# Every fourth attention head: V held still in TensorE, probabilities streamed past it

## The chip, the cores and the metric

The kernel runs on one core of one Trainium2 chip. The metric is the device time of one execution in microseconds, and the median of several executions is what is compared. TensorE does the matrix products, ScalarE (ACT) the exponentials, VectorE (DVE) the evacuations of PSUM and the elementwise work, GpSimd (POOL) a few scalars and some DMA issues, and SyncE (SP) most DMA issues.

## The reference

What is computed, cut to what matters here: a layer norm, an attention block over 32 heads with 2048 queries and 2048 cached keys, an MLP with a squared ReLU whose SiLU gates the attention's output, and a residual.

```python
xn = _layernorm(x)                        # x: 1 x 2048 x 512
q = (xn @ wq)                             # to 32 heads x 2048 x 128
scores = einsum("bhqd,bhkd->bhqk", q, k_cache) * (128 ** -0.5)
p = softmax(scores)                       # over 2048 keys
o = einsum("bhqk,bhkd->bhqd", p, v_cache)
s = o.reshape(1, 2048, 4096) @ wo         # to 512
h = relu(xn @ w1 + b1) ** 2               # 512 to 1792
g = silu(h @ w2 + b2)                     # back to 512
out = x + s * g
```

## The kernel before

**Tiling.** The 2048 queries are cut into 4 blocks of 512 (`QB`). A "group" g is one head of one block, so there are 128 groups (`NG`), g = 32 * block + head. The 2048 keys of a group are cut into 16 tiles of 128, taken two at a time: 8 "pairs" (`NPR`) a group, 1024 pairs (`NPAIR`) in all. One pass of the main loop (line 963) is one pair `pi`, called a step here.

**What one step puts on TensorE, in this order.** `gen_scores(pi)` (line 528): two matmuls of 512 columns, with a K tile stationary and the 512 queries moving, into one half of `psA`; behind them ACT's exponential of the 128x1024 result into `pT` (line 550 on), one of `NPT` = 4 buffers. Then none to three "fill" matmuls of 512 columns (`fill_one`, line 793): pieces of the Q projections, the MLP and the output projection, taken from a list of jobs in order of due step and paced by a credit, so that they last to the end. They go to the two banks of `psF`; a job's bank is evacuated by DVE, and two jobs later the bank is used again. Last, `gen_pv(pi - 2)` (line 559): the product of the probabilities with V, two steps behind the scores (`LAG`).

**The product with V before the change.** A pair takes 8 matmuls: for each of its two key tiles and each of 4 tiles of 128 queries, the 128x128 block of `pT` is the stationary operand and the V tile is the moving one. V has an extra column of ones (`Dh + 1` = 129 columns), so that column 128 of the result is the softmax's denominator. The 4 query tiles lie in two banks of `psO`, two to a bank. The helper `_mm_shared` (line 157) issues them; all other matmuls go through `_mm` (line 152). In a group's first and last pair the matmuls of bank 0 come before those of bank 1. After the last pair DVE copies the two banks to `o_un` (helper line 179), takes the reciprocal of the denominators (line 183), and multiplies into `o_bf` (line 165); `gen_oT` then has SP transpose `o_bf` by DMA into `oT`, which is what the output projection (`job_wo`) reads. `oT` has 24 slots (`NOT`).

**What orders the work.** All five instruction streams are written out by this program in order; each engine takes its own strictly in that order, and waits on counters of other engines and of DMAs. So an instruction on DVE that waits for something late holds all that is behind it on DVE. An exponential waits for its scores and for the product that last read its `pT` buffer. Scores of pair `pi` wait for the exponential of `pi - 2`, since `psA` holds two pairs. A group's first product into a bank of `psO` waits for that bank's copy.

**Layer norm of the next block.** `ln_transpose` (line 380) has SP transpose the normalised rows by DMA into `xnT`, which holds all 2048 queries.

```python
        if pi >= NPR:
            gen_pv(pi - LAG)
        if k == 0:
            fill_wq(g + 3)
            fill_k(g + 2)
        if k == LAG - 1:
            fill_v(g + 2)
        if k == LAG + 1 and g >= 1:
            gen_oT(g - 1)
```

Of the kernel before, what the change touches and what calls it, by code (L numbers as in the profile page):

```python
# [4 lines left out]

ACT = mybir.ActivationFunctionType
ALU = mybir.AluOpType
BF16 = mybir.dt.bfloat16
F32 = mybir.dt.float32
P = 128  # L10
# [193 lines left out]
    return e.bn_aggr(out, in_)  # L204


def _dma(e, out, in_):
    return e.dma_start(out, in_)  # L208

# [5 lines left out]
def bass_recurrent_scan__mha_block_cached__dense_activation_squared_relu__prompt_kernel(  # L215
# [13 lines left out]
    _, Sq, D = A_x.shape  # L229
# [3 lines left out]
    QB = 512  # L233
# [11 lines left out]
    HC = 8  # L245
# [12 lines left out]
    E = S.emit  # L258

    sb = nc.alloc_sbuf_tensor  # L260
    NSL, NSW, NQS, NPT, NOT = 3, 4, 3, 4, 3 * HC
    xnT = sb("xnT", [P, NDC, Sq], BF16)
    w1_sb = sb("w1_sb", [P, NDC, F], BF16)
    w2_sb = sb("w2_sb", [P, NFC, D], BF16)
    wo_all = sb("wo_all", [P, H, D], BF16)
# [9 lines left out]
    o_un = sb("o_un", [P, 2, TPB, Dh + 2], F32)  # L275
    rden = sb("rden", [P, 2, TPB], F32)
    o_bf = sb("o_bf", [P, 2, TPB, Dh], BF16)
    r_t = sb("r_t", [P, 2, QB], BF16)
    z_t = sb("z_t", [P, 2, D], F32)
    th_t = sb("th_t", [P, 2, D], BF16)  # L280
# [8 lines left out]
    ve_t = sb("ve_t", [P, TPB], F32)  # L289
    mhalf = sb("mhalf", [P, 1], F32)  # L290
    ident = sb("ident", [P, P], BF16)
    identf = sb("identf", [P, P], F32)
    warm = sb("warm", [P, P], BF16)
    rstd = sb("rstd", [P, TPB], F32)
    x_t = sb("x_t", [P, TPB, D], BF16)
    tmp_t = sb("tmp_t", [P, 2, D], F32)
    out_t = sb("out_t", [P, 2, D], BF16)

    psA = nc.alloc_psum_tensor("psA", [P, 4 * 512], F32)
# [6 lines left out]
    def bankO(i):  # L306
# [15 lines left out]
    sl_xt = [S.slot(f"xt{i}") for i in range(TPB)]  # L322
    sl_out = [S.slot("out0"), S.slot("out1")]
    sl_fin = [S.slot("fin0"), S.slot("fin1")]

    t_warm = E(GP, partial(_memset, out=warm[:], val=0.0))
    t_mhalf = E(GP, partial(_memset, out=mhalf[:], val=-0.5))
    t_idf = E(GP, partial(_iota, out=identf[:]))
    t_ident = E(GP, partial(_ts, out=ident[:], in0=identf[:], scalar1=0.0, scalar2=None,
                            op0=ALU.is_equal), deps=[t_idf])  # L330
    t_ones = None
    for i in range(NSL):
# [4 lines left out]


    t_xl = {}
    t_xn = {}  # L340
    t_xr = {}
    t_xnr = {}
# [37 lines left out]
    def ln_transpose(j, i):  # L380
        jt = j * TPB + i
        t_xnr[jt] = tok_xT[j][i] = S.emit_dma(
            SP, partial(_dmaT, out=xnT[:, :, jt * P:(jt + 1) * P], in_=xn_t[:, i, :]),
            sl_xT[i], deps=[t_xn[jt]])

    def ln_next(j, i):
        ln_scale(j, i)
# [140 lines left out]
    def gen_scores(pi):  # L528
        g, k = divmod(pi, NPR)
        s2, i = pi % 2, g % NSL  # L530
        assert t_kfill[g] is not None and t_evac[g] is not None
        t = None
        if g == 0:
            qt, b = divmod(pi, 2)
            for c in range(NKT // 2):
                t = E(PE, partial(_mm_shared, out=psA[:, s2 * 1024 + c * P:s2 * 1024 + (c + 1) * P],
                                  lhsT=kT[:, 0, (b * NKT // 2 + c) * P:(b * NKT // 2 + c + 1) * P],
                                  rhs=qt_sb[:, 0, qt * P:(qt + 1) * P], start=True, stop=True),
                      deps=[t_k0[b], t_q0[qt], t_exp[pi - 2] if pi >= 2 else t_b1[0]],
                      inc=(c == NKT // 2 - 1))  # L540
        else:
            for n in range(2):
                tt = 2 * k + n
                t = E(PE, partial(_mm, out=psA[:, s2 * 1024 + n * 512:s2 * 1024 + (n + 1) * 512],
                                  lhsT=kT[:, i, tt * P:(tt + 1) * P], rhs=qt_sb[:, g % NQS, :],
                                  start=True, stop=True),
                      deps=[t_exp[pi - 2] if pi >= 2 else None, t_kfill[g], t_evac[g],
                            t_bankF[0] if pi == 0 else None],
                      inc=(n == 1))
        if k == NPR - 1:  # L550
            t_S_last[g] = t
        t_exp[pi] = E(AC, partial(_act, out=pT[:, pi % NPT, :],
                                  in_=psA[:, s2 * 1024:(s2 + 1) * 1024],
                                  func=ACT.Exp, scale=SM_SCALE),
                      deps=[t, t_PV[pi - NPT] if pi >= NPT else None])

    t_bank = [None, None]

    def gen_pv(pi):
        g, k = divmod(pi, NPR)  # L560
        i = g % NSL
        last = k == NPR - 1
        if k == 0:
            t_bank[:] = [None, None]
        order = [(2 * k + n, qt, n * QB + qt * P) for n in range(2) for qt in range(TPB)]
        if last or k == 0:
            order = [(2 * k + n, qt, n * QB + qt * P) for b in range(2)
                     for qt in (2 * b, 2 * b + 1) for n in range(2)]
        if g == 0:
            order = [(k % 2 * (NKT // 2) + n, k // 2, n * P) for n in range(NKT // 2)]  # L570
        t = None
        for idx, (tt, qt, p0) in enumerate(order):
            b = qt // 2
            inc = idx == 7 or (last and g > 0 and idx == 3)
            t = E(PE, partial(_mm_shared, out=bankO(b)[:, qt % 2 * 256:qt % 2 * 256 + Dh + 1],
                              lhsT=pT[:, pi % NPT, p0:p0 + P],
                              rhs=v_sb[:, i, tt, 0:Dh + 1],
                              start=(tt == 0 and qt % 2 == 0), stop=(tt == NKT - 1)),
                  deps=[t_exp[pi], t_v0[k % 2] if g == 0 else t_vfill[g], t_ones,
                        t_evac[1] if g == 0 and b == 1 else None,  # L580
                        t_oev[g - 1][b] if g >= 1 else None], inc=inc)
            if inc:
                t_bank[b] = t
        t_PV[pi] = t
        if last:
            t_PV_last[g] = t
            s = g % 2
            for b in range(2):
                t_oev[g][b] = E(DV, partial(_copy, out=o_un[:, s, 2 * b:2 * b + 2, 0:Dh + 1],
                                            in_=bankO(b).rearrange("p (s c) -> p s c", s=2)[:, :, 0:Dh + 1]),  # L590
                                deps=[t_bank[b], t_onorm[g - 2] if g >= 2 else None])
            tr = E(DV, partial(_recip, out=rden[:, s, :], in_=o_un[:, s, :, Dh]),
                   deps=[t_oev[g][0], t_oev[g][1], t_onorm[g - 2] if g >= 2 else None])
            base = rden[:, s, :]
            rb = bass.AP(tensor=base.tensor, offset=base.offset,
                         ap=[list(base.ap[0]), [1, TPB], [0, Dh]])
            t_onorm[g] = E(DV, partial(_tt, out=o_bf[:, s, :, :], in0=o_un[:, s, :, 0:Dh], in1=rb,
                                       op=ALU.mult),
                           deps=[tr, tok_oT[g - 2] if g >= 2 else None])

    def gen_oT(g):
        tok_oT[g] = S.emit_dma(
            SP, partial(_dmaT, out=oT[:, g % NOT, :].rearrange("p (t q) -> p t q", q=P),
                        in_=o_bf[:, g % 2, :, :].rearrange("p t d -> p (t d)")), sl_oT[g % 4],
            deps=[t_onorm[g], t_wodone[g - NOT] if g >= NOT else None])
# [12 lines left out]
    t_zrd = [None, None]  # L618
    t_thr = [None, None]
    events = {}  # L620
    nfin = [0]

    pending = []
# [3 lines left out]

    def job_proj(g):
        j = g // H
        js = slice(j * QB, (j + 1) * QB)  # L630
        i = g % NSW

        def mm(n, bank):
            t = E(PE, partial(_mm, out=bankF(bank), lhsT=wq_sb[:, i, n, :], rhs=xnT[:, n, js],
                              start=(n == 0), stop=(n == NDC - 1)),
                  deps=[t_wqfill[g], t_bankF[bank]] + tok_xT[j], inc=(n == NDC - 1))
            assert t_wqfill[g] is not None and None not in tok_xT[j]
            if t is not None:
                t_proj[g] = t

        def evac(bank, step):
            t_evac[g] = E(DV, partial(_copy, out=qt_sb[:, g % NQS, :], in_=bankF(bank)),
                          deps=[t_proj[g], t_S_last[g - NQS] if g >= NQS else None])
            return t_evac[g]
        return NDC, mm, evac

    def job_h(j, c):
        js = slice(j * QB, (j + 1) * QB)
        box = [None]

        def mm(n, bank):
            box[0] = E(PE, partial(_mm, out=bankF(bank), lhsT=w1_sb[:, n, c * P:(c + 1) * P],
                                   rhs=xnT[:, n, js], start=(n == 0), stop=(n == NDC - 1)),
                       deps=[tok_w1[c // 2], t_bankF[bank]] + tok_xT[j], inc=(n == NDC - 1))

        def evac(bank, step):
            s = c % 2
# [305 lines left out]
    for pi in range(NPAIR):  # L963
# [17 lines left out]
            n += 1  # L981
        if pi >= NPR:
            gen_pv(pi - LAG)
        if k == 0:
            fill_wq(g + 3)
            fill_k(g + 2)
# [17 lines left out]
        step += 1  # L1004
    while tail_order:
        tail_one(step)
    assert not jobs and cur[0] is None and not events and not pending

    fin = [_Tok(sl.sem, sl.val) for sl in sl_out + sl_fin]
    S.emit_wait(SP, fin)  # L1010
# [29 lines left out]
```

The softmax here doesn't subtract the row's maximum and nothing guards it: scores larger than these inputs give would overflow.

## Time and profile before

| what | value |
|---|---|
| median of 4 runs | 1238.13 us (1237.68 to 1238.33) |
| the profiled execution | 1238.26 us, span 1236.5 us |
| exponentials, 128x1024 | 1024 of 1024 ns each |
| products with V, 129 columns | 8192 matmuls |
| score matmuls, 512 columns | 2032 (and 64 of 128 columns at the start) |
| fill matmuls, 512 columns | 504 + 480 + 224 + 224 in `psF`, 16 at the end in `psA` |
| tanh on ACT, 128x512 | 16, 622 ns each |
| load on the 16 DMA engines | 80.4% of 16 engines by the queue that SP, mostly, feeds; 1.1% by POOL's |

How to read it: TensorE's records are modelled at their ends and overlap (a 512-column matmul has 379 ns in the records), so its cost is read from the distance between starts. The span covers the instructions; the execution's own time is 1.8 us longer. A group lasts about 1236.5 / 128 = 9.66 us and a step 1.21 us.

### The profile page before, as it was taken

To read this page: it belongs to the slowest core of one execution; us is meant where nothing else is said; L and a number is where in the kernel's file an instruction comes from. 1 tells how busy PE (TensorE), PEld (TensorE's weight loads), DVE (VectorE), ACT (ScalarE), POOL (GpSimd) and SP (SyncE) were. 2 spreads that over 40 slices of the span, in tenths; PEclk is the share of its full clock that TensorE was granted. 3 is DMA by queue.
4 is the path that set the end of the run, shared out by engine and by line. 5 is a ranking of instruction groups with operands and counts; after the bars stand their busy time and mean duration, and the time that the engine had idled before them with its cause. 6 is when DMAs were issued, how large, how long until landed. Compare 5 with 4: busy or idle time off the path is not lost.

```text
span 1236.5 us, 26934 instructions
## 1 busy us (share of the span) xinstructions
PE 1232.1 (100%) x11885; PEld 819.5 (66%) x11885; DVE 472.7 (38%) x953; ACT 1054.6 (85%) x1044; POOL 32.0 (3%) x73
## 2 busy tenths in 40 slices
PE   9999999999999999999999999999999999999999
PEld 7666666666666666666666666666666666666665
DVE  4453323244435332334444532333344333324333
ACT  7888888888888888888888888888888888888885
POOL 1010000000002000000000200000000000000000
DMA  9999998677879898767778888787778789878761
GB/s 210 206 233 202 187 179 134 130 144 142 141 151 173 142 158 131 140 139 145 134 132 171 171 139 143 141 148 134 133 146 148 146 154 158 137 135 146 145 122 31
DMA packets 686868, 185.41 MB, mean 150 GB/s; under 512 B 673536, under 2 KB 685568, under 8 KB 686752
## 3 DMA queue, kind: packets, MB, share of 16 engines
q1 hardware_dynamic: 684656, 179.62, 80.4%
q0 software_dynamic: 1424, 3.81, 1.1%
q8 instruction: 94, 1.54, 0.6%
q10 hardware_dynamic: 672, 0.26, 0.1%
q14 instruction: 22, 0.18, 0.1%
HBM read 96.60 MB, written 2.10 MB: 80 GB/s over the span
## 4 chain that ended last, share of the span: by engine, by line
PE 99%; DMA 0%; DVE 0%; issue 0%; SPq 0%; DVEq 0%
PE psO L157 38%; PE psA L152 36%; PE psF L152 25%; DMA kT<-in_A_k_cache_dram 0%; PE psA L157 0%; PE psO L196 0%; DVE out_t L165 0%; PE psF L196 0%; DVE tmp_t L175 0%; PE psO L152 0%; DVE xnT L179 0%; SPq L208 0%; PE psA L196 0%; DVEq L119 0%
## 5 line engine op out<-in xcount | busy, mean ns | idle before, releaser
L161 ACT ACTIVATE pT<-psA 128x1024 bf16<-128x1024 f32 x1024 | 1044.5, 1024 | 162.5 <-PE psA L152 117.6
L157 PEld LDWEIGHTS psO<-v_sb,pT 128*128 128x128 bf16 x8192 | 547.9, 98 | 240.2 <-issue 12.4
L157 PE MATMUL psO<-v_sb,pT 128*128 128x129 bf16 x8192 | 631.2, 220 | 0.0
L152 PE MATMUL psA<-qt_sb,kT 128*128 128x512 bf16 x2032 | 604.4, 379 | 0.0
L179 DVE COPY o_un<-psO 128x258 f32<-128x258 f32 x256 | 97.4, 422 | 399.4 <-PE psO L157 398.7
L152 PE MATMUL psF<-xnT,wq_sb 128*128 128x512 bf16 (+1 forms) x520 | 168.8, 374 | 0.1
L152 PE MATMUL psF<-wo_all,oT 128*128 128x512 bf16 x480 | 163.7, 379 | 0.0
L152 PEld LDWEIGHTS psA<-qt_sb,kT 128*128 128x128 bf16 x2032 | 157.0, 98 | 0.0
L179 DVE CAST qt_sb<-psF 128x512 bf16<-128x512 f32 (+1 forms) x130 | 88.0, 677 | 97.5 <-PE psF L152 97.5
L165 DVE TENSOR_TENSOR o_bf<-o_un,rden 128x512 bf16<-128x512 f32 x128 | 88.6, 692 | 4.6 <-DVE rden L183 0.3
L152 PEld LDWEIGHTS psF<-xnT,wq_sb 128*128 128x128 bf16 x520 | 50.3, 98 | 59.8 <-DVE xnT L179 0.2
L171 DVE TENSOR_SCALAR r_t<-psF,b1f 128x512 bf16<-128x512 f32 x56 | 42.0, 750 | 117.5 <-PE psF L152 117.5
L152 PEld LDWEIGHTS psF<-wo_all,oT 128*128 128x128 bf16 x480 | 46.9, 98 | 56.4
L152 PE MATMUL psF<-xnT,w_sb 128*128 128x512 bf16 x224 | 77.1, 379 | 0.0
L152 PE MATMUL psF<-w_sb,h2T 128*128 128x512 bf16 x224 | 74.1, 379 | 0.0
L152 PEld LDWEIGHTS psF<-w_sb,h2T 128*128 128x128 bf16 x224 | 21.9, 98 | 26.4
L152 PEld LDWEIGHTS psF<-xnT,w_sb 128*128 128x128 bf16 x224 | 21.9, 98 | 26.4
L165 DVE TENSOR_TENSOR z_t<-psF,b2bc 128x512 f32<-128x512 f32 x16 | 11.1, 692 | 67.2 <-PE psF L152 67.2
L165 DVE TENSOR_TENSOR acc<-psF,acc 128x512 f32<-128x512 f32 x28 | 19.3, 689 | 30.0 <-PE psF L152 30.0
L208 POOL DMA_DIRECT2D out_dram<-out_t x12 | 6.7, 557 | 891.0 <-DVE out_t L165 891.0
L165 DVE TENSOR_TENSOR h2T<-r_t 128x512 bf16<-128x512 bf16 x56 | 23.8, 425 | 1.9
L183 DVE RECIPROCAL rden<-o_un 128x4 f32<-128x4 f32 x128 | 22.9, 179 | 4.4
(47 smaller groups left out, 166.3 us busy)
## 6 DMA issues: line engine op xcount, KB each, us to landing
v_sb<-in_A_v_cache_dram SPq DMA_DIRECT2D x127, 512.0 KB, 4.7
wq_sb<-in_A_wq_dram SPq DMA_DIRECT2D x127, 128.0 KB, 3.0
wo_all<-in_A_wo_dram SPq DMA_DIRECT2D x4, 1024.0 KB, 6.2
w_sb<-in_B_w_dram SPq DMA_DIRECT2D x14, 256.0 KB, 4.8
oT<-o_bf SPq DMA_TRANSPOSE x128, 4.0
x_t<-in_A_x_dram POOLq DMA_DIRECT2D x16, 128.0 KB, 3.2
kT<-in_A_k_cache_dram SPq DMA_TRANSPOSE x127, 4.5
x_ln<-in_A_x_dram SPq DMA_DIRECT2D x15, 128.0 KB, 4.3
```

The lines of the kernel that those rows point to most:

```text
L152: return e.matmul(out, lhsT, rhs, start=start, stop=stop)
L157: return e.matmul(out, lhsT, rhs, start=start, stop=stop, skip_group_check=True)
L161: return e.activation(out, in_, func, bias=bias, scale=scale)
L165: return e.tensor_tensor(out, in0, in1, op)
L171: return e.tensor_scalar(out, in0, scalar1=scalar1, scalar2=scalar2, op0=op0, op1=op1)
L179: return e.tensor_copy(out, in_)
L183: return e.reciprocal(out, in_)
L208: return e.dma_start(out, in_)
```

## The change

Of the 128 groups, those with `g % 4 == 1` and `4 < g < 126` are handled in a second way ("B groups" here, the others "A groups"): g = 5, 9, ..., 125, which are 31. Both ways compute the same.

In a B group a pair's product takes 2 matmuls: the V tile (128 columns, no ones) is stationary, and 512 probabilities of `pT` move past it. The result is o transposed, 128x512, in bank 0 of `psO` alone. ACT copies it to `o_un`. The denominators are not in it any more: DVE reads every `pT` pair of the group with a reduction that transposes 32x32 blocks (`den_part`, 8 a group, 128x1024 each), sums the parts (`den_sum`), writes 128x16 sums to DRAM over POOL's DMA queue, reads them back by 4 DMAs so that each group of 32 partitions holds all four quarters, sums these, takes the reciprocal and spreads it by a DVE transpose (`den_spread`), and multiplies into `oT` directly (`den_scale`). There is no DMA transpose of `o_bf` for a B group.

`plan_b` fixes the steps after whose product these are emitted: the parts at steps 8g + 2 + (0, 1, 3, 4, 6, 7, 9, 10), the sum at 8g + 14, the spread at 8g + 21, the scaling at 8g + 22. The group after a B group does its first pair's bank 0 products one step later, between the bank 1 and the bank 0 products of its second pair. There are 8 `pT` buffers in place of 4, and an exponential also waits for the part that reads its buffer. `xnT` holds two blocks in place of four (its DMA transposes then wait for the last use of the block before last), and `identf` lies in `tmp_t`.

```diff
-    NSL, NSW, NQS, NPT, NOT = 3, 4, 3, 4, 3 * HC
-    xnT = sb("xnT", [P, NDC, Sq], BF16)
+    NSL, NSW, NQS, NPT, NOT = 3, 4, 3, 8, 3 * HC
+    xnT = sb("xnT", [P, NDC, 2 * QB], BF16)
...
+    def is_b(g):
+        return g % 4 == 1 and 4 < g < NG - 2
...
-            sl_xT[i], deps=[t_xn[jt]])
+            sl_xT[i], deps=[t_xn[jt], t_xuse.get(j - 2)])
...
-                      deps=[t, t_PV[pi - NPT] if pi >= NPT else None])
+                      deps=[t, t_PV[pi - NPT] if pi >= NPT else None, t_part.get(pi - NPT)])
...
+    def gen_pv_b(pi):
+        g, k = divmod(pi, NPR)
+        i = g % NSL
+        for n in range(2):
+            tt = 2 * k + n
+            t_PV[pi] = E(PE, partial(_mm, out=bankO(0), lhsT=v_sb[:, i, tt, 0:Dh],
+                                     rhs=pT[:, pi % NPT, n * QB:(n + 1) * QB],
+                                     start=(tt == 0), stop=(tt == NKT - 1)),
+                         deps=[t_exp[pi], t_vfill[g], t_free[0]], inc=(n == 1))
+        if k == NPR - 1:
+            t_PV_last[g] = t_PV[pi]
+            t_free[0] = E(AC, partial(_act, out=o_b(g), in_=bankO(0), func=ACT.Copy),
+                          deps=[t_PV[pi], t_onorm[g - 2]])
...
+    def den_part(pi):
+        k = pi % NPR
+        t_part[pi] = E(DV, partial(_reduce_t, out=d_part[:, k, :],
+                                   in_=pT[:, pi % NPT, :].rearrange("p (b j) -> p b j", j=32)),
+                       deps=[t_exp[pi], t_den[0]])
+
+    def den_sum(g):
+        t_den[0] = E(DV, partial(_reduce, out=d_sum[:],
+                                 in_=d_part[:].rearrange("p k (n b) -> p b (k n)", n=2)),
+                     deps=[t_part[NPR * (g + 1) - 1], t_den[1]])
+        t_den[1] = S.emit_dma(GP, partial(_dma, out=d_scr, in_=d_sum[:]), sl_dw,
+                              deps=[t_den[0], t_den[2]])
+        src = bass.AP(tensor=d_scr.tensor, offset=d_scr.offset,
+                      ap=[[NBK, 32], [32 * NBK, 4], [1, NBK]])
+        free = [t_den[1], t_den[3]]
+        for a in range(4):
+            t_den[2] = S.emit_dma(GP, partial(_dma, out=d_quad[32 * a:32 * (a + 1), :, :],
+                                              in_=src), sl_dr, deps=free)
+
+    def den_spread(g):
+        t_den[3] = E(DV, partial(_reduce, out=d_rec[:],
+                                 in_=d_quad[:].rearrange("p a b -> p b a")),
+                     deps=[t_den[2], t_den[5]])
+        t_den[4] = E(DV, partial(_recip, out=d_rec[:], in_=d_rec[:]), deps=[t_den[3]])
...
+        t_den[5] = E(DV, partial(_transpose32, out=r_all[:], in_=spread),
+                     deps=[t_den[4], t_den[5]])
+
+    def den_scale(g):
+        t_onorm[g] = tok_oT[g] = E(
+            DV, partial(_tt, out=oT[:, g % NOT, :], in0=o_b(g),
+                        in1=r_all[:].rearrange("p b i -> p (b i)"), op=ALU.mult),
+            deps=[t_free[0], t_den[5], t_wodone[g - NOT] if g >= NOT else None])
+
+    def plan_b(g):
+        first = NPR * g + LAG
+        for k in range(NPR):
+            at_once.setdefault(first + 3 * k // 2, []).append(partial(den_part, NPR * g + k))
+        at_once.setdefault(first + 12, []).append(partial(den_sum, g))
+        at_once.setdefault(first + 19, []).append(partial(den_spread, g))
+        at_once.setdefault(first + 20, []).append(partial(den_scale, g))
...
+        if after_b and k == 0:
+            later[:] = order[:4]
+            order = order[4:]
+        if after_b and k == 1:
+            order = [x for x in order if x[2] >= 2] + later + [x for x in order if x[2] < 2]
...
+        if k == 0 and is_b(g):
+            plan_b(g)
+        for fn in at_once.pop(pi, []):
+            fn()
```

The helpers `_reduce_t` and `_reduce` are `tensor_reduce` with an add over the last axis, the first with `apply_transpose=True`; `_transpose32` is DVE's `transpose`.

## The prediction

> **What bounds the kernel now.** I read the page's busy shares first, then the chain that ended last, then the timeline of TensorE.
>
> ```profile
> span 1236.5 us, 26934 instructions
> ...
> PE 1232.1 (100%) x11885; PEld 819.5 (66%) x11885; DVE 472.7 (38%) x953; ACT 1054.6 (85%) x1044; POOL 32.0 (3%) x73
> ...
> PE 99%; DMA 0%; DVE 0%; issue 0%; SPq 0%; DVEq 0%
> ```
>
> TensorE never stops, and the chain that set the end is 99% TensorE. So two things alone can move the time: fewer TensorE nanoseconds, or a new wait on TensorE. For the nanoseconds I need the pitch from start to start, since records overlap. This is TensorE's timeline late in the run (start us, length us, engine, line, operation, tiles, shape, count):
>
> ```profile
> 1208.77 0.59 PE L152 MATMUL psA<-qt_sb,kT 128*128 128x512 bf16 x2
> 1209.20 0.38 PE L152 MATMUL psF<-wo_all,oT 128*128 128x512 bf16 x1
> 1209.41 0.62 PE L157 MATMUL psO<-v_sb,pT 128*128 128x129 bf16 x8
> 1209.87 0.59 PE L152 MATMUL psA<-qt_sb,kT 128*128 128x512 bf16 x2
> 1210.30 0.62 PE L157 MATMUL psO<-v_sb,pT 128*128 128x129 bf16 x8
> 1210.75 0.59 PE L152 MATMUL psA<-qt_sb,kT 128*128 128x512 bf16 x2
> ```
>
> Two score matmuls take 1209.20 - 1208.77 = 0.43 us, one fill 0.21, eight products 0.455. Over the 13 steps from 1206.56 to 1220.23 there are 36 matmuls of 512 columns and 104 of 129: at 0.2158 us for the first, the second come to (13.67 - 7.77) / 104 = 0.0567 us. Check: 8192 x 0.0567 + some 3,490 x 0.2158 = 1218 us, and the start and the end make up the rest. Weight loads (98 ns each) are hidden at both pitches.
>
> **The gain.** A pair of a B group drops 8 x 0.0567 = 0.4536 us and adds 2 x 0.2158 = 0.4316 (the price of the score matmuls, the same shape with a new weight load each): 0.022 us. Times 8 pairs it is 0.176 us a group, times 31 groups **5.5 us**. The two pairs after a B group are only reordered. [...]
>
> So 0.176 us a group is the whole stake: a wait of that size on TensorE in each B group eats it. The rest is a search for waits.
>
> **DVE's new work.** Its rows:
>
> ```profile
> L179 DVE COPY o_un<-psO 128x258 f32<-128x258 f32 x256 | 97.4, 422 | 399.4 <-PE psO L157 398.7
> L165 DVE TENSOR_TENSOR o_bf<-o_un,rden 128x512 bf16<-128x512 f32 x128 | 88.6, 692 | 4.6 <-DVE rden L183 0.3
> ...
> L183 DVE RECIPROCAL rden<-o_un 128x4 f32<-128x4 f32 x128 | 22.9, 179 | 4.4
> ...
> L200 DVE BATCH_NORM_STATS2 st_t<-x_ln 128x6 f32<-128x512 bf16 x15 | 10.2, 682 | 3.5 <-DMA x_ln<-in_A_x_dram 3.5
> ...
> L200 DVE BATCH_NORM_STATS2 st_t<-x_ln 128x6 f32<-128x256 bf16 x2 | 0.8, 420 | 0.0
> ```
>
> Removed in a B group: 2 x 0.422 + 0.179 + 0.692 = 1.71 us. Added: the part, a reduction over 1024 bf16 elements with a transpose, has no row. The nearest is the statistics row, also a reduction: (682 - 420) / 256 = 1.02 ns an element, so 0.682 + 512 x 1.02 = 1.21 us. The lower bound is two elements at a time, by the bf16 row of `xn_t` (406 ns for 512): about 0.7 us; the upper, that the transpose halves the rate: 2.25. I take 1.21. Eight make 9.7; the sum over 256 elements 0.42 (the 256 row), over 64 some 0.22, reciprocal 0.18, transpose and scaling of 512 as the 692 row each. Sum 11.9, net +10.2 us a group, x 31 = 315: DVE goes from 473 to about 788 us (64%). That it hides rests on three places. [...]
>
> *The `pT` buffers.* Part 0 can start when the group before is normalised, at about step 8g + 3.3. The exponential of pair 8g + 15 waits for part 7, at about step 8g + 15.5: 12.2 steps x 1.2 us = 14.6 us for eight parts and some 2 us of other DVE work. Records on DVE overlap by 0.08 us (two copies of 0.42 take 0.76), so 8 x 1.13 + 2 = 11 us: 3.6 us to spare.
>
> *Evacuations behind a part.* From the end of a `psF` evacuation to the first matmul that needs that bank again the trace has at least 0.94 us, and over 1.8 us in 19 of 20. A part holds one back by at most 1.13 us, mostly less, since the parts run ahead of their places whenever DVE has nothing to wait for. `psO` copies are tighter: bank 1's end only 0.14 us before its next use. But A copies are emitted at steps 8g + 1, 8g + 17, 8g + 25, and between part 7 (8g + 12) and 8g + 17 DVE catches up. I allow 0.4 us over the whole run.
>
> *The trip through DRAM.* POOL's rows:
>
> ```profile
> L208 POOL DMA_DIRECT2D x_t<-in_A_x_dram x16: 538/538/616, 89.1 to 1015.8; - x16
> ...
> DMA to landing us min/median/max: 2.3/3.2/5.1
> ```
>
> POOL's writes to `out` land in 2.0 to 4.0 us, median 2.3. Write 2.3, handoff 0.1, the fourth read issued 3 x 0.54 = 1.6 later, landing 3.2: 7.2 us; bounds 5.9 and, with 4.0 and 5.1, 10.8. Packets of 64 bytes have no row; `b1b`, 3.5 KB, took 4.7, which for both ends makes 11.1. From the sum to the spread there are 7 steps, 8.4 us. If it is late, DVE stands at the spread. The next evacuation behind it (step 8g + 22, ready at 22.9) has 8.9 x 1.2 = 10.7 us from the sum's step, less 0.4 for the sum and 1.6 for spread and scaling, plus 1.8 slack: 10.5. The copies of group g + 2, at the end of step 8g + 25, give (11.9 x 1.2) - 2.0 = 12.3. So it is covered, with a margin of 3 to 5 us. POOL's other work (layer norm scalars 30 steps ahead of use, output issues) can bear that wait. For g = 125 the last fill of the loop, which reads this `oT` slot, runs in step 1023 (1220.66 us in the trace), one step after the scaling; DVE is idle there for 6.5 us, so parts and sum come early.
>
> **ACT's new work.** One copy of 128x512 from PSUM a B group, between two exponentials. The trace has the same insertion sixteen times, the tanh:
>
> ```profile
> 1195.09 1.02 ACT L161 ACTIVATE pT<-psA 128x1024 bf16<-128x1024 f32 x1 [0.29 <-PE psA L152]
> 1196.01 0.62 ACT L161 ACTIVATE th_t<-z_t 128x512 bf16<-128x512 f32 x1
> 1196.53 1.02 ACT L161 ACTIVATE pT<-psA 128x1024 bf16<-128x1024 f32 x1
> ```
>
> It holds the next exponential by 0.52 us, which ends at 1197.55; TensorE starts the scores that need it at 1197.97, with no gap. Over the sixteen the least slack left is 0.33 us. The copy's product is done before the exponential in front of it ends. ACT rises by 31 x 0.62 = 19 us to 1074 (87%). If the cover were gone, 0.52 x 31 = 16 us.
>
> **Moved and dropped.** SP loses 31 DMA transposes of `oT` and gains nothing; a transpose of `xnT` now waits for uses that ended some 80 steps before. `oT` of a B group is there at 8g + 23, the earliest output job that reads it is released 16 steps on. These cost nothing.
>
> **The sum.** 1238.26 (the profiled execution; the median is 0.13 lower) - 5.5 + 0.4 = 1233.2; against the median **1233.0 us**. The floor is the gain with no wait, 1232.6, less run scatter: 1232.0.
>
> **Rivals.** A measurement of this kernel can tell about 0.2% (2.5 us) from no change.
>
> *Small waits eat it* (0.13). Evacuations behind parts, or the ACT copy, cost about 0.1 to 0.25 us a group: 31 x 0.18 = 5.5, so 1236 to 1240, middle 1238. For: the `psO` copies have 0.14 us. Against: the schedule keeps parts off those steps, and the tanh rows.
>
> *The parts are too slow* (0.06, slower). Place: the exponential of pair 8g + 15, held by part 7; its point is 8c + 2 = 14.6 + 0.5 of slack, c = 1.6 us a part. At 2.25 it is 8 x 0.65 = 5.2 us a group, 161 us: 1394. For: no transposing row. Against: the statistics row is 0.4 us below the point.
>
> *The DRAM trip* (0.08, slower). DVE stands at the spread until the reads land; it decides from 10.5 to 12.3 us. At 14 us it costs (14 - 12.3) x 31 = 53: 1285. For: `b1b`'s 4.7 us, and the DMA engines are 80% busy with large loads. Against: every loaded POOL row in mid-run is under 5.1.
>
> *The change doesn't save* (0.02, slower). The V loads are not hidden: 16 x 0.098 x 31 = 49 us, 1281. Against: the score matmuls do just that at 216 ns.
>
> **Numbers.** The forecast has 0.71, and it is all of "faster" (below 1235.65); small waits make "same", 0.13; the other three "slower", 0.16. The range runs from 1232.0 into the small waits, to 1238.5; about 0.2 lies above. The forecast's own range is 1232.0 to 1235.
>
> **What would show it.** Right: TensorE's idle still none, products of B groups at 216 ns start to start, 10,397 matmuls, DVE near 788 us with parts near 1.2 us each, 31 ACT copies of about 0.62, and from sum to landing of the reads about 7 us. Wrong: an exponential waiting for a part, a weight load of `psA` or `psF` waiting for DVE, or DVE waiting for `d_quad` for microseconds with a `psO` copy behind it.

## The result, and the profile after

The changed kernel takes 1239.38 us in the median of 41 runs (1238.03 to 1244.13), against 1237.84 us of 61 runs before (1237.67 to 1238.53). The ratio is 1.0016, with a 95% interval of 1.0011 to 1.0020: no faster, by a hair slower, 6.4 us above the forecast of 1233.0 and 0.9 us above its range. The profiled execution took 1240.11 us. Its page begins so (span, busy time and share of each engine), and its chain of waits is no longer TensorE's alone:

```profile
span 1238.3 us, 24563 instructions
...
PE 1227.5 (99%) x10397; PEld 755.2 (61%) x10397; DVE 770.0 (62%) x1232; ACT 1063.4 (86%) x1075; POOL 118.1 (10%) x228
...
PE 88%; DVE 6%; DMA 4%; issue 1%; POOL 1%; SPq 0%; DVEq 0%
```

These are shares of the chain's length, followed back through each wait; what TensorE lost is far less and is counted below. The table of waits (engine and line, what it waited for: total us, times, longest) says where DVE and the DMAs come in. In the trace of before no such line stands:

```profile
DVE d_rec L209 <- DMA d_quad<-d_scr: 45.6, 20, 4.7
...
PE psO L158 <- DVE o_un L180: 4.9, 5, 1.3
...
PE psF L153 <- DVE oT L166: 1.3, 1, 1.3
```

DVE stands at the spread (`d_rec<-d_quad`) in 20 of 31 B groups, 46 us together, until the reads from DRAM land. In five groups the `psO` copies behind it come so late that TensorE waits, and once the last fill of the loop waits for `oT`. Taken from start to start of the matmuls, the six waits are 1.00, 1.50, 1.49, 0.63, 1.11 and 1.43 us, with a few small ones 7.3 us. Set against the span before: 1236.5 - 5.5 + 7.3 = 1238.3. So the whole gain is there, and it is paid back.

The groups of instructions of the changed kernel (line, engine, operation, tiles, count, busy us, mean ns):

```profile
L153 PE MATMUL psO<-pT,v_sb 128*128 128x512 bf16 x496 | 147.5, 379 | 0.0
...
L213 DVE TRANSPOSE_TENSOR_REDUCE d_part<-pT 128x32 f32<-128x1024 bf16 x248 | 291.8, 1217 | 0.0
...
L217 DVE STREAM_TRANSPOSE r_all<-d_rec 128x512 f32<-128x512 f32 x31 | 22.1, 712 | 1.1
...
L162 ACT ACTIVATE o_un<-psO 128x512 f32<-128x512 f32 x31 | 18.3, 591 | 0.0
L209 DVE TENSOR_REDUCE d_sum<-d_part 128x16 f32<-128x256 f32 x31 | 18.0, 580 | 0.5
```

A part costs 1217 ns, the copy on ACT 591, the products of a B group follow each other at 216 ns (379 is the modelled record). But for the sum (580 ns, taken as 420) the prices of the work were right. What failed is the time at which one result is there.

How one wait comes about is seen in group 25. This is DVE's timeline (start us, length us; in brackets the idle time before, and what ended it):

```profile
261.83 1.23 DVE L213 TRANSPOSE_TENSOR_REDUCE d_part<-pT 128x32 f32<-128x1024 bf16 x1
262.99 0.65 DVE L176 SCALAR_TENSOR_TENSOR acc<-acc,g_all 128x512 f32<-128x512 f32 x1
263.67 0.69 DVE L166 TENSOR_TENSOR acc<-acc,x_t 128x512 f32<-128x512 f32 x1
264.28 0.68 DVE L180 CAST qt_sb<-psF 128x512 bf16<-128x512 f32 x1
264.88 0.57 DVE L209 TENSOR_REDUCE d_sum<-d_part 128x16 f32<-128x256 f32 x1
...
274.98 0.26 DVE L209 TENSOR_REDUCE d_rec<-d_quad 128x16 f32<-128x64 f32 x1 [3.39 <-DMA d_quad<-d_scr]
...
276.19 0.65 DVE L176 SCALAR_TENSOR_TENSOR acc<-acc,g_all 128x512 f32<-128x512 f32 x1
276.88 0.69 DVE L166 TENSOR_TENSOR acc<-acc,x_t 128x512 f32<-128x512 f32 x1
277.49 0.68 DVE L180 CAST qt_sb<-psF 128x512 bf16<-128x512 f32 x1
278.09 0.68 DVE L166 TENSOR_TENSOR oT<-o_un,r_all 128x512 bf16<-128x512 f32 x1
278.87 0.76 DVE L180 COPY o_un<-psO 128x258 f32<-128x258 f32 x2
```

Between part 7 and the sum stand three instructions of other jobs, 1.9 us. Then the sum, and the trip: POOL issues the write at 265.75, it lands 3.3 us later, and four reads go out, as POOL's timeline shows:

```profile
265.75 0.56 POOL L221 DMA_DIRECT2D d_scr<-d_sum  x1 [34.38 <-DVE d_sum L209]
269.36 2.18 POOL L221 DMA_DIRECT2D d_quad<-d_scr  x4 [3.05 <-DMA d_scr<-d_sum]
```

The last read lands 4.0 us after its issue, 9.5 us after the sum's end. Behind the spread again three instructions of other jobs, and only then the scaling and the copies, at 278.87. TensorE's timeline shows the price: the products that these copies read (the first line) had ended by 277.46 in the records, and the next ones come after a gap of 1.5 us more than the fill's own 0.216 from start to start:

```profile
276.84 0.62 PE L158 MATMUL psO<-v_sb,pT 128*128 128x129 bf16 x8
277.30 0.59 PE L153 MATMUL psA<-qt_sb,kT 128*128 128x512 bf16 x2
277.73 0.38 PE L153 MATMUL psF<-wo_all,oT 128*128 128x512 bf16 x1
279.44 0.65 PE L158 MATMUL psO<-v_sb,pT 128*128 128x129 bf16 x8 [1.34 <-DVE o_un L180]
```

### The profile page after: what moved, and what is told of

Same layout as the page of the kernel before. It is cut to its first block, busy times and chain, and to the rows that moved or that the text cites. A ratio compares the mean times of both kernels' runs of the same rounds, so it can differ in the third digit from the quotient of the medians.

```text
span 1238.3 us, 24563 instructions
## 1 busy us (share of the span) xinstructions
PE 1227.5 (99%) x10397; PEld 755.2 (61%) x10397; DVE 770.0 (62%) x1232; ACT 1063.4 (86%) x1075; POOL 118.1 (10%) x228
## 4 chain that ended last, share of the span: by engine, by line
PE 88%; DVE 6%; DMA 4%; issue 1%; POOL 1%; SPq 0%; DVEq 0%
PE psA L153 32%; PE psO L158 25%; PE psF L153 23%; PE psO L153 8%; DVE d_part L213 2%; DMA d_quad<-d_scr 2%; DMA d_scr<-d_sum 2%; POOL d_quad L221 1%; DVE qt_sb L180 0%; DVE r_t L172 0%; DMA kT<-in_A_k_cache_dram 0%; DVE acc L166 0%; DVE o_un L180 0%; DVE oT L166 0%; DVE h2T L166 0%
## 5 line engine op out<-in xcount | busy, mean ns | idle before, releaser
L158 PEld LDWEIGHTS psO<-v_sb,pT 128*128 128x128 bf16 x6208 | 414.8, 98 | 187.6 <-issue 14.0
L158 PE MATMUL psO<-v_sb,pT 128*128 128x129 bf16 x6208 | 478.2, 220 | 4.9 <-DVE o_un L180 4.9
L213 DVE TRANSPOSE_TENSOR_REDUCE d_part<-pT 128x32 f32<-128x1024 bf16 x248 | 291.8, 1217 | 0.0
L180 DVE COPY o_un<-psO 128x258 f32<-128x258 f32 x194 | 73.8, 421 | 210.2 <-PE psO L158 209.5
L153 PEld LDWEIGHTS psA<-qt_sb,kT 128*128 128x128 bf16 x2032 | 167.1, 98 | 58.6
L153 PE MATMUL psO<-pT,v_sb 128*128 128x512 bf16 x496 | 147.5, 379 | 0.0
L221 POOL DMA_DIRECT2D d_scr<-d_sum x31 | 17.5, 564 | 892.9 <-DVE d_sum L209 892.9
L153 PEld LDWEIGHTS psO<-pT,v_sb 128*128 128x128 bf16 x496 | 48.5, 98 | 58.6 <-issue 2.8
L221 POOL DMA_DIRECT2D d_quad<-d_scr x124 | 67.9, 554 | 69.1 <-DMA d_scr<-d_sum 65.8
L166 DVE TENSOR_TENSOR o_bf<-o_un,rden 128x512 bf16<-128x512 f32 x97 | 67.1, 692 | 3.8 <-DVE rden L184 0.5
```

The costliest lines, as they stand in the source:

```text
L153: return e.matmul(out, lhsT, rhs, start=start, stop=stop)
L158: return e.matmul(out, lhsT, rhs, start=start, stop=stop, skip_group_check=True)
L166: return e.tensor_tensor(out, in0, in1, op)
L180: return e.tensor_copy(out, in_)
L213: return e.tensor_reduce(out, in_, axis=AX.X, op=ALU.add, apply_transpose=True)
```

## The experiments

Two theories stood against each other. T: only the lateness of the trip through DRAM costs. R: DVE's 10 us of new work a B group are too much by themselves. All times are medians; the kernel before ran beside each on the same chip, at 1237.9 to 1238.0 us.

**Take the wait away.**

```diff
+    t_quad = E(GP, partial(_memset, out=d_quad[:], val=512.0))
...
-            t_den[2] = S.emit_dma(GP, partial(_dma, out=d_quad[32 * a:32 * (a + 1), :, :],
+            t_den[2] = S.emit_dma(GP, partial(_dma, out=d_land[32 * a:32 * (a + 1), :, :],
...
-                     deps=[t_den[2], t_den[5]])
+                     deps=[t_quad, t_den[5]])
```

> The four reads land in a tile that nobody uses and the spread reads a constant, so all DMAs run as in the change but DVE never waits for them (left out: the true denominators of the B groups). Theory T (the trip through DRAM is late, DVE stands at the spread, and the copies of group g + 2 and the last oT come late): no wait on TensorE in mid-run, 5.5 us below before, near 1232.4 us. Rival R (DVE's 10 us a B group are too much by themselves, evacuations come late behind the parts whether or not the trip is late): TensorE still waits, 1236.5 us or more.

Measured: 1232.72 us (1232.43 to 1233.12), ratio 0.9958 (0.9945 to 0.9971). TensorE has no new wait in mid-run. DVE is as busy as in the change (769 us), so R falls at every fourth head, and the gain of 5.5 us is confirmed to 0.3 us. Busy time and chain of its profile:

```profile
PE 1225.9 (100%) x10397; PEld 754.3 (61%) x10397; DVE 769.2 (63%) x1232; ACT 1062.6 (86%) x1075; POOL 117.8 (10%) x229
...
PE 99%; DMA 0%; DVE 0%; SPq 0%; issue 0%; DVEq 0%
```

**Leave g = 125 out.**

```diff
-        return g % 4 == 1 and 4 < g < NG - 2
+        return g % 4 == 1 and 4 < g < NG - 6
```

> The last B group, g = 125, is made an A group again (30 B groups). T: the 1.43 us wait before the last fill of the loop goes, 0.18 us of gain goes with it: 1.2 us below the change, near 1238.2 us; the five waits in mid-run stay. R, or if the end has another limit behind this one: within 0.3 us of the change.

Measured: 1246.91 us (1244.73 to 1246.95), ratio 1.0067 (1.0055 to 1.0079): a miss by 8.7 us. The wait before the last fill did go, and the five in mid-run stayed (8.4 us together in this trace, where the longest trips took 11.5 us). But 5.8 us of the span lie behind the last store: POOL's closing DRAIN took 10.5 us. The experiments with more DMAs, below, are about that.

**Start the trip earlier.**

```diff
-        at_once.setdefault(first + 12, []).append(partial(den_sum, g))
+        at_once.setdefault(first + 10, []).append(partial(den_sum, g))
```

> The sum is emitted right behind part 7 (step 8g + 12 in place of 8g + 14), nothing else moves. T, and that the trip starts late where other DVE work stands between part 7 and the sum: groups whose sum began at 8g + 15 or later start up to 1.4 steps earlier, their waits (two or three of the five) go, 3 to 4 us below the change: near 1236 us; g = 125 has nothing between and keeps its wait. R: no difference over 0.5 us.

Measured: 1234.98 us (1233.64 to 1235.99), ratio 0.9975 (0.9965 to 0.9985). Nothing but the place of one short reduction is changed, and the median falls by 4.4 us: as T has it. In the trace one wait of 0.23 us is left in mid-run (g = 101), and the one of 1.49 us before the last fill, 1.7 us in place of 7.3. The trips are no shorter, 8.6 us in the median and up to 12.7 (g = 9), and DVE still stands at the spread in 17 groups; it only seldom matters any more:

```profile
DVE d_rec L209 <- DMA d_quad<-d_scr: 30.0, 17, 3.5
```

**Read back with one DMA.**

```diff
-        t_den[1] = S.emit_dma(GP, partial(_dma, out=d_scr, in_=d_sum[:]), sl_dw,
+        t_den[1] = S.emit_dma(GP, partial(_dma, out=bass.AP(
+            tensor=d_scr.tensor, offset=d_scr.offset, ap=[[NBK, 4], [4 * NBK, 32], [1, NBK]]),
+            in_=d_sum[:]), sl_dw,
...
-                      ap=[[NBK, 32], [32 * NBK, 4], [1, NBK]])
+                      ap=[[0, 4], [4 * NBK, 32], [1, 4 * NBK]])
...
-        for a in range(4):
-            t_den[2] = S.emit_dma(GP, partial(_dma, out=d_quad[32 * a:32 * (a + 1), :, :],
-                                              in_=src), sl_dr, deps=free)
+        t_den[2] = S.emit_dma(GP, partial(_dma, out=d_quad[:].rearrange("p a b -> p (a b)"),
+                                          in_=src), sl_dr, deps=free)
```

> The sums are written to DRAM in another order so that one DMA reads them back in place of four; the work on DVE is the same. T: the last read is issued 1.6 us earlier, the trip falls from a median of 8.6 to about 7 us, and since the five waits in mid-run were 0.6 to 1.5 us, nearly all go, the last one too: 1233 to 1234 us. R: no difference, 1239 us.

Measured: 1242.6 us in the median of 12 runs from 1236.32 to 1244.56, ratio 1.0029 (1.0018 to 1.0041): a miss. The trace, which is of the fastest run, has four waits, 3.8 us, in groups that wait in the change too, and none at the end. The trip fell only from 8.6 to 8.1 us in the median: the write took 3.0 us in place of 2.0 and the read 4.2 in place of 3.4, which gives back most of the 1.6 us saved at the issue. What the other runs lost has no profile.

**Both of these together.**

```diff
-        at_once.setdefault(first + 12, []).append(partial(den_sum, g))
+        at_once.setdefault(first + 10, []).append(partial(den_sum, g))
```

(on top of the kernel with one read)

> The two edits of e3_sum_early and e4_one_read together, still on POOL's queue (92 DMAs on it). T: no waits in mid-run, none at the last fill: 1232.5 to 1233 us on TensorE's side, and runs within 1 us. If the spread of e4_one_read (1236.3 to 1244.6 us) came from POOL's closing drain and not from late trips, runs above 1236 us stay.

Measured: 1232.53 us (1232.52 to 1232.81), ratio 0.9956 (0.9943 to 0.9970). With the trip started earlier the runs lie within 0.3 us, so the spread of the kernel with one read came with its late start. By what way is not shown. POOL's closing DRAIN (the experiments on it are below) was 2.95 us in the traces of both, but the trace of the kernel with one read is of its fastest run. In nine of its twelve runs the mean granted clock was 0.997 to 0.999, and in the two kernels of this section with a drain of 10.5 us it is 0.998, so a long drain in its other runs is not excluded.

**Move the trip to SP.**

```diff
+    def den_trip(g):
+        t_den[1] = S.emit_dma(SP, partial(_dma, out=bass.AP(
+            tensor=d_scr.tensor, offset=d_scr.offset, ap=[[NBK, 4], [4 * NBK, 32], [1, NBK]]),
+            in_=d_sum[:]), sl_dw, deps=[t_den[0], t_den[2]])
...
+        t_den[2] = S.emit_dma(SP, partial(_dma, out=d_quad[:].rearrange("p a b -> p (a b)"),
+                                          in_=src), sl_dr, deps=free)
...
+        at_once.setdefault(first + 10, []).append(partial(den_sum, g))
+        at_once.setdefault(first + 13, []).append(partial(den_trip, g))
```

> The trip moves from POOL's queue to SP's: the sum right behind part 7, then one write and one read issued by SP at step 8g + 15, ahead of the loads that SP issues at 8g + 16. Theory T (only the lateness of the trip costs): the reads land before step 8g + 20, TensorE has no wait over 0.2 us, all of the 5.5 us come through: 1232.5 us, and the runs lie within 1 us of each other. If SP's own loads suffer from the wait in front of them, the next K or V load is late: TensorE waits for a K or V load, over 1234 us.

Measured: 1232.42 us (1232.31 to 1232.81), ratio 0.9955 (0.9943 to 0.9968). Its profile is the forecast's: DVE's load of the change, and a chain that is TensorE's again. DVE never waits for `d_quad`. Three things are changed here at once: the queue, the earlier sum and the one read. The kernel above has the last two on POOL's queue and takes 1232.53 us, so the queue by itself brought 0.1 us at most, which is within the scatter of the runs; what it does is to give slack, since DVE still stood at the spread 16 times there (13.9 us).

```profile
PE 1226.4 (100%) x10397; PEld 755.4 (61%) x10397; DVE 770.7 (63%) x1232; ACT 1063.3 (86%) x1075; POOL 31.9 (3%) x73
...
PE 99%; DVE 0%; issue 0%; POOL 0%; DVEq 0%; POOLq 0%
```

**More B groups on top of that.** Three choices, by the condition in `is_b` alone:

```diff
-        return g % 4 == 1 and 4 < g < NG - 2
+        return g % 2 == 1 and 4 < g < NG - 2
```

> As e5_trip_on_sp, with every second head from 5 to 125 a B group (61 in place of 31). T: 61 x 0.176 = 10.7 us, 1227.2 us, if DVE (some 88% busy) still evacuates in time. Rival R (DVE's load is the limit, only not yet at every fourth): evacuations and parts come late, TensorE waits, more than 1232.5 us.

Measured: 1238.38 us (1238.02 to 1238.8), ratio 1.0003 (0.9994 to 1.0012). DVE is busy 1049 us (85%), and TensorE waits 10.4 us together. Here R holds, with the wait that the prediction's second rival named, exponentials that wait for a part, and with evacuations behind parts:

```profile
ACT pT L162 <- DVE d_part L213: 17.5, 21, 2.2
...
PE psA L153 <- ACT pT L162: 5.0, 8, 1.6
...
PE psF L153 <- DVE r_t L172: 2.2, 3, 1.5
```

The waits stand close together: behind groups 7, 39 and 71 (where the statistics of the next block's layer norm are taken) and around 27 to 31 of a block.

```diff
-        return g % 4 == 1 and 4 < g < NG - 2
+        return g % 3 == 1 and 4 < g < NG - 2
```

> As e5_trip_on_sp, with every third head from 7 to 124 a B group (40). Each B group is worth 0.176 us if nothing waits: 7.0 us below before, 1230.9 us (T, DVE about 69% busy). R, by e6_every_second (10.4 us of waits with 61, by the parts at the steps of the layer norm and of the output projection): waits of a microsecond or more, 1232 us or above.

Measured: 1232.12 us (1232.03 to 1232.46), ratio 0.9953 (0.9941 to 0.9965). Nine groups more than on SP with every fourth should bring 1.6 us and brought 0.3. An exponential waits for a part four times (2.7 us), which TensorE feels once for 0.7 us; where the other 0.6 us went is not known. DVE is busy 859 us (70%).

```diff
+        return g % 2 == 1 and g % 32 not in (7, 29, 31) and 4 < g < NG - 2
```

> As e6_every_second without the groups g % 32 = 7, 29 and 31, behind which nearly all of its 10.4 us of waits stood (layer norm statistics of the next block; accumulation of the output): 50 B groups. If those waits are local to these groups, 50 x 0.176 = 8.8 us: 1229.2 us plus up to 1 us. If they come from DVE's total load, they move elsewhere: 1232 us or more.

Measured: 1230.10 us (1229.86 to 1231.09), ratio 0.9938 (0.9925 to 0.9950), the fastest version here. Leaving out 11 of 61 groups takes 8.3 us off. DVE's total falls with them, from 85% to 77%, and no run leaves out 11 other groups, so that the waits belong to these groups is made likely and not shown. For it speaks that the kernel with every third head, whose DVE is less busy (70%) but which keeps g = 7, 31, 61 and 103 of these groups, falls short of its price by as much, 1.2 us (7.0 less 5.8) against 1.0 here (8.8 less 7.8).

**POOL's closing drain.** First the kernel without g = 125, with five DMAs more that nobody waits for:

```diff
+        for a in range(4):
+            t_den[2] = S.emit_dma(GP, partial(_dma, out=d_land[32 * a:32 * (a + 1), :, :],
+                                              in_=src), sl_dr, deps=[t_den[1]])
...
+        if g == 121:
+            at_once.setdefault(1014, []).append(idle_trip)
```

> As e2_not_125, with a write and four reads on POOL's queue at the place of g = 125 that nobody waits for. The profile of e2_not_125 ended 5.8 us after SP was done, with POOL's closing DRAIN (10.5 us there, 4.65 in the change). If the drain depends on how many DMAs POOL issued, or on how long ago the last was, it is 4 to 5 us here and the time falls from 1246.9 to about 1241; if not, it stays near 1246.9.

Measured: 1239.09 us (1236.97 to 1239.84), ratio 1.0006 (0.9997 to 1.0015): 7.8 us below the same kernel with five DMAs fewer. The drain is 4.66 us in place of 10.5; the rest is that the waits in mid-run are 6.0 us in this trace, in place of 8.4.

Then the kernel before, with trips that nobody waits for and nothing else of the change:

```diff
+        if k == 6 and g % 4 == 2 and 4 < g < NG - 4:
+            idle_trip(g - 1)
```

> The kernel before, with 30 trips (150 DMAs) on POOL's queue at the steps of the change that nobody waits for and nothing else. T: TensorE has no wait, and what the time does is the drain at the end alone: 1238.0 if it ends within 4.5 us, 1243 to 1244 if it takes 10.5 us as in e2_not_125. Rival: the small DMAs hold up the loads of K, V and Q weights, TensorE waits for loads in mid-run.

Measured: 1243.64 us (1243.5 to 1244.2), ratio 1.0046 (1.0032 to 1.0060), with no wait on TensorE in mid-run. So the small DMAs hold up no load that TensorE needs; all 5.7 us are the drain. One trip more (`4 < g < NG`):

> As e8_before_dmas with one more trip, at step 1014: POOL issues 185 DMAs as in the change, in place of 180. In the four traces with 185 the closing drain took 4.66 us and in the two with 180 it took 10.5. If the length goes with the number issued, the drain is 4.66 us here, ends with SP, and the time is 1238.0 to 1238.5; if it goes with when they are issued or with the kernel around, it stays near 1243.6.

Measured: 1238.01 us (1237.73 to 1238.62), ratio 0.9999 (0.9990 to 1.0009). These are the lines of POOL's sequencer from the view of the closing block, first with 180 DMAs on POOL's queue (count, duration in ns as least, median and most, start in us), and when SP is done:

```profile
L134 POOLq DRAIN  x1: 10533/10533/10533, 1231.0 to 1231.0; - x1
...
L134 SPq DRAIN  x1: 7/7/7, 1235.7 to 1235.7; - x1
```

and with 185:

```profile
L134 POOLq DRAIN  x1: 4657/4657/4657, 1231.9 to 1231.9; - x1
...
L134 SPq DRAIN  x1: 7/7/7, 1236.6 to 1236.6; - x1
```

With 180 POOL ends 5.8 us after SP, with 185 together with it.

## Why the prediction was wrong

**Right: what bounds, the gain, and each price.** The pitch of 57 and 216 ns held: in the trace of the change eight products of an A group take 0.45 us (1212.01 to 1212.46) and two of a B group 0.43 (65.26 to 65.69), and 5.5 us is what the kernels without waits gained (1237.95 - 1232.42 = 5.5 on SP, 5.3 without the wait). A part was put at 1.21 us and took 1.217; ACT's copy at 0.62, 0.59; DVE at 788 us, 770. The sum's reduction over 256 elements was too low, 0.42 against 0.58 us. The `pT` buffers, the evacuations behind parts and ACT cost nothing measurable at every fourth head, as argued: the kernel without the wait shows it.

**Wrong: "So it is covered, with a margin of 3 to 5 us."** The place was right and stood among the rivals at 0.08: DVE at the spread, and the copies of group g + 2 behind it. The point from which it decides was put at 10.5 to 12.3 us of trip, where the trip itself was taken as 7.2. The trips were longer, but none in this trace reached that point (the longest took 10.1 us): the point itself was too late as well. Three terms of the budget were mis-sized, and they add up in the same groups:

- The trip, from the end of the sum to the last landing, took 6.6 to 10.1 us over the 31 groups, 8.6 in the median. The bounds, 5.9 to 11.1, held in this trace (not in every kernel: see the 12.7 and 11.5 us above); the value taken did not. Each of the two handoffs on POOL, before the write and before the reads, took 0.3 us, where one of 0.1 had been taken, and the last of the four reads landed 3.7 us after its issue in the median. The landing of all reads, as the view of their tile gives it (least, median and most), had been taken as 3.2:

```profile
DMA to landing us min/median/max: 1.8/3.4/5.6
```

- The start. The budget ran from step 14. Where the accumulation of the output (two instructions, 1.3 us) and a cast stand between part 7 and the sum, the sum began as late as step 15.7 (g = 25, 57, 117), up to 2.1 us after TensorE had begun step 14. The experiment that moves the sum in front of that work, and nothing else, got back 4.4 us.
- What is queued behind the spread. The budget held spread and scaling alone, 1.6 us. In group 25 there are 3.9 us from the landing to the copies: 1.2 for the spread, 1.9 for two accumulations and a cast of other jobs, 0.7 for the scaling.

For group 25, counted from TensorE's first score matmul of step 14: 1.9 us until the sum begins, 0.6 for the sum, 9.5 of trip, 3.9 behind it, together 15.9 us until the copies. Step 26, whose products need them, begins 14.3 us after step 14. The rest, 1.6 us, is the 1.5 that TensorE waited. The same for the five groups that TensorE waited for (all in us; in step 26 scores and fills come ahead of the product, so it can wait less than the copies are late). In the other groups the copies began within 0.2 us of the start of step 26 or before it.

| g | sum late | trip | landing to copies | sum of these and the sum's 0.6 | step 14 to step 26 | TensorE waited |
|---|---|---|---|---|---|---|
| 5 | 0.8 | 10.1 | 3.9 | 15.4 | 14.1 | 1.00 |
| 25 | 1.9 | 9.5 | 3.9 | 15.9 | 14.3 | 1.50 |
| 57 | 2.1 | 9.5 | 3.9 | 16.1 | 14.5 | 1.49 |
| 97 | 1.0 | 10.1 | 3.1 | 14.8 | 13.9 | 0.63 |
| 101 | 1.7 | 9.9 | 3.1 | 15.3 | 14.1 | 1.11 |

No one of the three would have been enough: with the prediction's values for the other two, the largest start gives 2.1 + 0.6 + 7.2 + 1.6 = 11.5 us, the longest trip 0.6 + 10.1 + 1.6 = 12.3, and the longest queue behind in these groups 0.6 + 7.2 + 3.9 = 11.7, all under 13.9. That is arithmetic on the trace; the runs show it for the start (moved) and for the wait as a whole (taken away).

**Wrong: "DVE is idle there for 6.5 us, so parts and sum come early"**, for g = 125. The trace before shows DVE idle there (6.46 us, until TensorE's products end), but the parts fill that idle time: six in a row, and the sum began at step 14.6. POOL then issued the reads 2.2 us after the write had landed (0.3 in all other groups; by the profile it waited for nothing, so why is open), and the last fill waited 1.43 us for the scaling:

```profile
1220.84 0.59 PE L153 MATMUL psA<-qt_sb,kT 128*128 128x512 bf16 x2
1222.70 0.39 PE L153 MATMUL psF<-wo_all,oT 128*128 128x512 bf16 x1 [1.27 <-DVE oT L166]
```

**The rivals.** The size that came, a loss of a quarter of a microsecond a group on average, is that of "small waits eat it"; the mechanism is that of the DRAM trip. That rival was priced as if the budget were exceeded in every group alike, 31 us for each microsecond. In fact only five groups, where other DVE work stands both before and behind the trip, exceed it by more than 0.2 us, and the last one at the end; that is why the loss was 7.3 us in the trace and not 50. The parts were not too slow (1.217 us, against a point of 1.6), and the V loads, 98 ns each, were hidden at 216 ns a product.

## What to carry to other kernels

When a result goes through DRAM to an engine that works in order, count its budget from when the producer's instruction can really start, with all that is queued ahead of it, to when the consumer's last dependent instruction is through, with all that is queued behind it; the largest group decides, not the median one. Where a change trades a few tenths of a microsecond per stage on the bounding engine, move such a trip off the place where it can be late at all: here one line's step was worth 4.4 us and, with one read in place of four, 6.9 us, while the new form of the product gains 5.5. And before a form is spread to more stages, look at which stages share the helper engine: 50 chosen groups gained 7.8 us, 61 gained nothing.

## What the runs showed that was not expected

POOL's closing DRAIN goes in these 14 traces with the number of DMAs that POOL had issued, but not in proportion: 3.83 us with 30 (five traces: before, and the four with the trip on SP), 2.95 with 92 (the two with one read on POOL's queue), 10.53 with 180 (two) and 4.66 with 185 (five), to 0.02 us the same in quite different kernels. With 180 it set the end of the execution and cost 5.7 us of a kernel that was otherwise the one before. It does not follow the time since the last of them, as far as that was varied: with 185 that was 15 us before the DRAIN in the change and 41 us in the kernel without g = 125 and with five DMAs more, and both DRAINs took 4.66 us. Why the length goes so was not found. The granted clock of TensorE fell to 0.64 in the last 5 us of the kernel without g = 125, while only POOL was still draining, which goes with the mean of 0.998 there:

```profile
1236.00:1240.00 4.00, 0.35 (x7) 0.17 (x4) 1.17 (x4) 0.00 (x0) 0.00 (x0) 1.00 0.22 66
1240.00:1245.00 5.00, 0.00 (x0) 0.00 (x0) 0.00 (x0) 0.00 (x0) 0.00 (x0) 0.64 0.00 0
```

(the columns are the stretch in us, its length, busy us and counts of PE, its weight loads, DVE, ACT and POOL, the clock, the DMA share and GB/s). In three runs of the kernel with one read (1243.76 to 1243.90 us) the mean clock was as low, 0.997; whether TensorE stood idle there as well, and where, no profile shows.
